# An FFT convolution feeding a mixture of experts: float16 products two token sets earlier, scale loads reordered, second-layer weights split in other groups

## The chip, the core and the metric

The kernel runs on one core of a Trainium2 chip. The metric is the device time of one execution in microseconds; less is better. In the text PE is TensorE's matmul unit and PEld its weight load, DVE is VectorE, ACT is ScalarE, POOL is GpSimd and SP is SyncE, whose queue issues most transfers.

## The reference

A length-2496 real FFT along the sequence is multiplied by a filter and transformed back, for 8 batches of 256 channels. The 19968 rows that come out go through a top-2 mixture of 8 experts.

```python
X = np.fft.rfft(x, axis=1)                                   # x: 8 x 2496 x 256
y = np.fft.irfft(X * (filt_r + 1j * filt_i)[None], n=2496, axis=1)
x = y.reshape(19968, 256)
noisy = x @ w_gate + np.log1p(np.exp(x @ w_noise)) * noise    # 8 experts
top2 = the two largest of noisy; top2_w = softmax over these two
for e in range(8):
    for k in range(2):
        mask = top2[:, k] == e
        h = np.maximum(x[mask] @ w1[e], 0.0)                  # 256 -> 1024
        out[mask] += top2_w[mask, k, None] * (h @ w2[e])      # 1024 -> 256
```

All inputs and the output are float32.

## The kernel before

**Two streams in one program.** `fft_stream` is a generator that emits the FFT, gating and routing of the 8 batches in small steps. `expert` emits the expert products in blocks of 512 gathered rows, and yields 13 times in a block: once after each of the 8 groups `f` of hidden units, once when the next block has been prepared, and once after each of the 4 groups of 128 output rows. `run` puts the two together: after each yield of `expert` it lets `fft_stream` take some steps, by a pace for each set, and it lets the generator `wscales` take some steps too. A scheduler then orders the instructions of each engine by the order of the program and the availability that it computes; engines execute in that order.

**Sets and blocks.** Blocks come in sets; set i may only use the rows of batches 0 to i. `SETS` is 2, 12, 18, 24, 34, 44, 54, 64: set 0 is blocks 0 and 1, set 1 blocks 2 to 11, set 2 blocks 12 to 17, all single blocks with their own expert and weights (n = 1); set 3 is blocks 18 to 23, in pairs that share one expert's weights (n = 2), and so on. Smaller blocks and the prepared weights of the tail follow.

**Splitting a product in three.** Each float32 operand is split into a high and a low part, and `_mm3` (lines 124 to 126) makes three matmuls: high by high, high by low, low by high. A block has 8 groups x 2 halves of the inner dimension x 3 = 48 matmuls of 512 columns in the first layer (into `hps`) and 4 row groups x 8 x 3 = 96 matmuls of 256 columns in the second (into `yps`). Blocks with `ready < HALF` (`ready` is the set's number plus 1) split into parts of the type float32r, the others into scaled float16 parts:

```python
if ent[0][5] >= HALF:
    xT.append(self.pair(h, l, x, self.xs[ent[0][5]][:, 0:1]))   # float16, scaled
else:
    nc.scalar.copy(h, x)                                        # float32r
    nc.vector.tensor_sub(l, x, f32v(h))
```

For w1 the same choice stands in `wsplit` (lines 1316 with 1203 and 1204, or 1322 and 1323), for w2 in lines 1319 and 1320 or 1322 and 1323. With `HALF` at 5, blocks 0 to 23 use float32r and the rest float16.

**The scales** are powers of two. `wscales` finds the weights' scales: 64 loads of 256 KB (`load`, line 598) into two buffers `wp` in turn, each followed two steps later by an ACT instruction that sums squares (`top`, line 603) and, after each fourth, a DVE maximum. Then `powers` turns the sums into scales by a short chain of PE, DVE, PE and DVE (lines 558 to 575, then `wtab`). Then 12 loads of a part of the rows of batches 0 and 1 (`load_y`, line 615) into the same two buffers, with a DVE maximum each (line 620), for the activations' scale. `known` then lets `xscale` run in the FFT stream as soon as a batch is complete; a batch that comes earlier is put on the list `owed`. `run` spreads these 88 steps (`NPREP`) evenly over the first `READY` yields of `expert`, 280 of them, or 21.5 blocks. What is not done by the first float16 block is emitted there: `gather` copies that expert's scales on POOL (line 1149) ahead of the block's row gathers. POOL also scatters the results of the blocks (line 1399).

**w2** arrives in 4 quarters in the staging slots that w1 uses as well; in the first block that uses it each quarter is split on ACT and DVE in the groups f = 1, 3, 5 and 7, behind the group's relu (ACT, line 1371) and low part (DVE, line 1372).

Of the kernel before, what the change touches and what calls it, by code (L numbers as in the profile page):

```python
# [10 lines left out]
F32 = mybir.dt.float32  # L11
# [11 lines left out]
NB, S, D = 8, 2496, 256  # L23
# [110 lines left out]
PACES = 115  # L134
FILL = {0: 0, 1: 14}
RAW = 3
HALF = 5
EVERY = 3
SETS = FIRST + [18 + 2 * n for n in PAIRS[ALONE:]]
READY = 13 * SETS[HALF - 2] - 32  # L140
FIRSTS = 2
NPREP = 8 * E + 2 + 4 + 12 + 2 + 4

# [9 lines left out]
class Moe:  # L153
# [40 lines left out]
    def setup(self):  # L194
        tc, nc, io, cp = self.tc, self.nc, self.io, self.cp
        self.z = cp.tile([128, YW // 2], F32, name="z")
        nc.gpsimd.memset(self.z, 0.0)
        self.ident = cp.tile([128, 128], F32, name="ident")
        make_identity(nc, self.ident)
        self.cV = cp.tile([128, 128], F32, name="cf")  # L200
        hl = cp.tile([128, 732], R32, name="hl")
        self.small = cp.tile([128, 320], F32, name="small")
        self.half = cp.tile([128, 4 * LR + 2 * NG], F16, name="half")
        self.fr = cp.tile([128, 2, 20, 128], F32, name="fr")
        self.fi = cp.tile([128, 2, 20, 128], F32, name="fi")
        self.wg = cp.tile([128, 2, 32], F32, name="wg")
        self.sgn = cp.tile([64, 20], F32, name="sgn")


        self.stage = cp.tile([128, 4096 + 4 * YW], F32, name="stage")  # L210
        self.turns = {}
        self.F = [self.stage[:, 2560 * h:2560 * h + 2560].rearrange("p (k b) -> p k b", k=CB) for h in range(2)]
        cm = self.P.tile([128, 366], F32, name="cm", tag="tl", bufs=3)
        self.cm = cm
        self.rC, self.rM, self.rD = cm[:RP, 0:120], cm[:, 120:248], cm[:120, 248:365]
        self.hl = hl
        nc.vector.memset(self.wg, 0.0)
        self.cC = (hl[:RP, 0:120], hl[:RP, 120:240])
        self.cM = (hl[:, 240:368], hl[:, 368:496])
        self.cD = (hl[:120, 496:613], hl[:120, 614:731])  # L220
        sm = self.small
        self.tri, self.ones, self.key = sm[:, 0:128], sm[:, 128:256], sm[:, 256:264]
        self.lastok, self.iota = sm[:, 264:265], sm[:, 272:272 + SW]
        self.epart, self.ebase, self.eoff = sm[:, 304:305], sm[:, 305:306], sm[:, 306:314]
        self.base = cp.tile([128, E], F32, name="base")
        self.cnt = cp.tile([E, 1], F32, name="cnt")
        self.done = cp.tile([E, 1], F32, name="done")
        self.nblk = cp.tile([E, 1], F32, name="nblk")
        for t in (self.cnt, self.done, self.nblk):
            nc.vector.memset(t, 0.0)  # L230
        self.tab = cp.tile([1, 2, SW], F32, name="tab")
        self.ymax = cp.tile([128, 2 * NB, 6], F32, name="ymax")
        self.xm = cp.tile([128, 1], F32, name="xm")
        self.wmax = cp.tile([128, 2 * E], F32, name="wmax")
        self.wquart = cp.tile([128, 4], F32, name="wquart")
        self.wtab = cp.tile([128, 3, E], F32, name="wtab")
        nc.vector.memset(self.ymax, 0.0)
        self.xs, self.scaled, self.known, self.owed, self.relu = {}, False, False, [], None

        self.rank = [cp.tile([RP, n, E], F32, name=f"rank{n}") for n in (39, 38)]  # L240
        nc.vector.memset(self.rank[0][:, :17], 0.0)
        nc.vector.memset(self.rank[1][:, :16], 0.0)

        self.pre = [cp.tile([128, 4 + E], F32, name=f"pre{i}") for i in range(2)]
        for t in self.pre:
            nc.vector.memset(t[:, :4], 0.0)
# [331 lines left out]
    def xscale(self, bt):  # L578

        nc = self.nc  # L580
        if not self.known:
            self.owed.append(bt)
            return
        nc.vector.tensor_reduce(self.xm, self.ymax[:, :2 * bt + 2], axis=AX.XY, op=ALU.max)
        q = yield from self.powers(self.xm, 1, TX)
        t = self.xs[bt + 1] = self.cp.tile([128, 2], F32, name=f"xs{bt}")
        nc.vector.tensor_copy(t, q[:, :, 0])
        yield

    def wscales(self):  # L590


        nc, io, v = self.nc, self.io, self.nc.vector

        def load(i):
            t = self.P.tile([128, 512], F32, name="wp", bufs=2)
            with self.after(self.spw):
                nc.sync.dma_start(t, io["w1" if i < 4 * E else "w2"][i // 4 % E, i % 4])
            return t

        def top(i, t):
            with self.after(self.relu):
                nc.scalar.activation(t, t, AF.Square, accum_out=self.wquart[:, i % 4:i % 4 + 1])
            if i % 4 == 3:
                v.tensor_reduce(self.wmax[:, i // 4:i // 4 + 1], self.wquart, axis=AX.X, op=ALU.max)

        Y = [(bt, h, g) for bt in range(FIRSTS) for h in range(2) for g in range(0, NG, 8)]

        def load_y(i):
            bt, h, g = Y[i]  # L610
            t = self.P.tile([128, 8, 64], I32, name="wp", bufs=2)
            y = self.y[BLK + bt * ROWS:BLK + (bt + 1) * ROWS].rearrange("(p g) d -> p g d", p=RP)
            k = min(8, NG - g)
            with self.after(self.spw):
                nc.sync.dma_start(t[:RP, :k], y[:, g:g + k, 128 * h + 64:128 * h + 128])
            return t[:RP, :k].rearrange("p g w -> p (g w)").bitcast(BF16)

        def top_y(i, t):
            bt, h, g = Y[i]
            v.tensor_reduce(self.ymax[:RP, 2 * bt + h, g // 8:g // 8 + 1], t, axis=AX.X, op=ALU.max, apply_absolute_value=True)  # L620

        raw, cut = (t.rearrange("p h k d -> p (h k d)")[:, :4096].rearrange("p (s q f) -> p s q f", s=2, q=4) for t in (self.fr, self.fi))

        def load_all(i):
            nc.sync.dma_start(raw[:, i % 2], io["w1" if i < E else "w2"][i % E].rearrange("q p f -> p q f"))

        def split(i, q):
            a, e = i // E, i % E
            o = cut[:, i % 2].rearrange("p q f -> p (q f)").bitcast(F16).rearrange("p (q f) -> p q f", q=4)
            h, l, t = o[:, q, :512], o[:, q, 512:], raw[:, i % 2, q]  # L630
            nc.scalar.activation(h, t, AF.Copy, scale=self.wtab[:, a, e:e + 1])
            v.scalar_tensor_tensor(l, t, self.wtab[:, a, e:e + 1], h, op0=ALU.mult, op1=ALU.subtract)
            if q == 3:
                nc.sync.dma_start(self.wpl[e, a].rearrange("q p f -> p q f"), o)

        def pairs(first, then, n):
            old = []
            for i in range(n + 2):
                if i >= 2:
                    self.pin(then, *old.pop(0), hold=False)  # L640
                if i < n:
                    old.append((i, self.pin(first, i, hold=False)))
                yield

        yield from pairs(load, top, 8 * E)
        for a, t in enumerate((TW1, TW2)):
            q = yield from self.powers(self.wmax[:, a * E:a * E + E], E, t, True)
            v.tensor_copy(self.wtab[:, a], q[:, 0])
            if a == 0:
                v.tensor_copy(self.wtab[:, 2], q[:, 1])  # L650
            else:
                v.tensor_mul(self.wtab[:, 2], self.wtab[:, 2], q[:, 1])
            yield
        yield from pairs(load_y, top_y, len(Y))
        self.known = True
        while self.owed:
            yield from self.xscale(self.owed.pop(0))
        self.scaled = True
        yield
        self.pin(load_all, 0)  # L660
        yield
        for i in range(2 * E):
            if i + 1 < 2 * E:
                self.pin(load_all, i + 1)
            yield
            for q in range(4):
                self.pin(split, i, q)
                if q < 3:
                    yield
# [664 lines left out]
    def expert(self, parts, may, fill=None):  # L1334
# [5 lines left out]
        while self.ahead:  # L1340
# [3 lines left out]
            blk, i = ent[:2]  # L1344
            lt, n, nt, s, tabi, ready = blk
            w = 128 * nt
            w1, xT, w2st, sc = cur
            if i == 0:
                w2, adds = [], []
# [5 lines left out]
            for f in range(8):  # L1355
# [17 lines left out]
                if f == 4:  # L1373
                    self.early_l = v
                hh.append((h, l))
                if f % 2 and i == 0:
                    w2.append(self.wsplit(w2st[f // 2], "w2", sc))
                yield
            late = not self.ahead
            if late:  # L1380
# [146 lines left out]
```

## Time and profile before

| | |
|---|---|
| time, median of 3 runs | 2170.51 us (2169.66 to 2174.63) |
| the profiled execution's own time | 2164.38 us |
| its span, first to last instruction | 2162.5 us |
| mean granted TensorE clock | 0.991 of full speed |
| PE busy | 2095.9 us, 97% |
| PEld busy | 1595.5 us, 74% |
| DVE busy | 1466.3 us, 68% |
| ACT busy | 1286.1 us, 59% |
| POOL busy | 1029.2 us, 48% |

The profile is of one execution. A matmul's recorded duration overlaps the next one's, so PE at 97% says that matmuls follow each other almost without a break; how fast they follow is read from the distance of their starts. "Idle before" an instruction is idle time of its engine, with what ended it. Times of rows below count from the span's start.

### The profile page before, as it was taken

The page shows a single profiled execution, that of the slowest core. Times are in us where ns is not written, and L with a number is a line of the kernel's source. Part 1 is how long each engine was busy: PE and PEld are TensorE (multiplying, and loading weights), DVE is VectorE, ACT ScalarE, POOL GpSimd, SP SyncE. Part 2 cuts the span into 40 slices and gives each one's busy share as a digit, 9 for nine tenths or more (in the row PEclk, how much of TensorE's full clock was granted, in tenths as well). Part 3 has the DMA queues.
Part 4 walks back from the last instruction along what each step waited for, and adds up shares of the span by engine and source line. Part 5 has one row for each costly group of instructions (what it writes and reads, how often), then busy time and mean ns, then how long its engine had stood idle before and what let it go on. Part 6 is the DMA issues. An engine that isn't in the chain of part 4 may idle for free. (4 is left out here: it accounts for less than half of the span.)

```text
span 2162.5 us, 42794 instructions
## 1 busy us (share of the span) xinstructions
PE 2095.9 (97%) x14517; PEld 1595.5 (74%) x14517; DVE 1466.3 (68%) x3221; ACT 1286.1 (59%) x2505; POOL 1029.2 (48%) x946
## 2 busy tenths in 40 slices
PE   8779999999999999999999999999999999999997
PEld 6447988888888888766766676666666666667886
DVE  5866779877978886678665986589666664333443
ACT  6666866786577446656664565555566564333443
POOL 4233334434544344445444453555655665654563
PEclk9989999999999999999999999999999999999999
DMA  9588989999999775767766687666889999869997
GB/s 255 165 259 223 222 223 215 252 228 228 223 214 233 161 156 137 178 150 183 155 156 131 152 182 165 146 121 132 233 210 240 240 249 234 170 142 229 276 280 175
DMA packets 511673, 428.48 MB, mean 198 GB/s; under 512 B 215679, under 2 KB 397015, under 8 KB 511447
## 3 DMA queue, kind: packets, MB, share of 16 engines
q1 hardware_dynamic: 450135, 341.27, 60.2%
q0 software_dynamic: 61312, 84.40, 23.1%
q8 instruction: 116, 1.90, 0.4%
q14 instruction: 110, 0.90, 0.1%
HBM read 263.92 MB, written 122.03 MB: 178 GB/s over the span
## 5 line engine op out<-in xcount | busy, mean ns | idle before, releaser
L1372 DVE SCALAR_TENSOR_TENSOR hl<-hps,hh 128x512 f16<-128x512 f32 (+3 forms) x712 | 432.4, 623 | 356.6 <-ACT hh L1371 354.7
L1399 POOL DMA_INDIRECT out<-stage,ids x316 | 532.9, 1686 | 270.4 <-ACT stage L1398 167.0
L1158 POOL DMA_INDIRECT stage<-y,ids x316 | 347.9, 1101 | 535.7 <-DMA xt<-stage 433.9
L124 PE MATMUL yps<-w,hh 128*128 128x256 f16 (+1 forms) x2048 | 556.5, 278 | 5.2 <-ACT stage L1398 3.4
L125 PE MATMUL yps<-w,hh 128*128 128x256 f16 (+1 forms) x2048 | 551.2, 277 | 0.0
L126 PE MATMUL yps<-w,hl 128*128 128x256 f16 (+1 forms) x2048 | 541.9, 277 | 1.8 <-DVE hl L1372 1.5
L1371 ACT ACTIVATE hh<-hps 128x512 f16<-128x512 f32 (+3 forms) x712 | 376.7, 550 | 198.9 <-PE hps L126 183.8
L125 PE MATMUL hps<-mxl,w1h 128*128 128x512 f16 (+1 forms) x1024 | 394.4, 386 | 2.2 <-DVE mxl L1246 1.3
L126 PE MATMUL hps<-mxh,w1l 128*128 128x512 f16 (+1 forms) x1024 | 394.0, 386 | 0.0
L124 PE MATMUL hps<-mxh,w1h 128*128 128x512 f16 (+1 forms) x1024 | 385.6, 388 | 5.1 <-DVE hl L1372 5.1
L1398 ACT ACTIVATE stage<-yps,gt 128x256 f32<-128x256 f32 x316 | 143.1, 475 | 329.0 <-PE yps L126 202.0
L124 PEld LDWEIGHTS <-hh 128*128 128x128 f16 x1760 | 172.2, 98 | 52.4 <-issue 6.2
L126 PEld LDWEIGHTS <-hl 128*128 128x128 f16 x1760 | 171.5, 98 | 47.9 <-DVE hl L1372 1.9
L125 PEld LDWEIGHTS <-hh 128*128 128x128 f16 x1760 | 172.2, 98 | 34.2 <-issue 2.6
L124 PEld LDWEIGHTS yps<-w,hh 128*128 128x128 f32 x768 | 145.8, 190 | 12.5 <-ACT stage L1398 2.2
L126 PEld LDWEIGHTS yps<-w,hl 128*128 128x128 f32 x768 | 145.0, 190 | 10.3 <-issue 1.7
L125 PEld LDWEIGHTS yps<-w,hh 128*128 128x128 f32 x768 | 145.4, 191 | 4.6
L126 PEld LDWEIGHTS <-w1l 128*128 128x128 f16 x640 | 62.6, 98 | 71.8 <-issue 1.5
L541 ACT COPY yt<-q 117x1024 uint16<-117x1024 uint16 x96 | 90.9, 947 | 40.7 <-PE q L535 32.1
L1228 DVE COPY stage<-xt 128x1024 uint16<-128x1024 uint16 (+2 forms) x174 | 109.0, 679 | 1.4 <-DMA xt<-stage 1.4
L124 PEld LDWEIGHTS <-w1h 128*128 128x128 f16 x640 | 62.4, 98 | 51.5 <-issue 5.5
L125 PEld LDWEIGHTS <-w1h 128*128 128x128 f16 x640 | 62.6, 98 | 51.1 <-issue 3.0
(286 smaller groups left out, 4024.4 us busy)
## 6 DMA issues: line engine op xcount, KB each, us to landing
stage<-w SPq DMA_DIRECT2D x328, 256.0 KB
x<-x SPq DMA_DIRECT2D x88, 256.0 KB
fd<-c SPq DMA_DIRECT2D x77, 240.0 KB
fi<-wpl SPq DMA_DIRECT2D x18, 1024.0 KB
fx<-fd SPq DMA_DIRECT2D x140, 128.0 KB
out<-z SPq DMA_DIRECT2D x24, 702.0 KB
wp<-w SPq DMA_DIRECT2D x64, 256.0 KB
fr<-w SPq DMA_DIRECT2D x16, 1024.0 KB
```

Source lines behind the costliest of these rows:

```text
L124: nc.tensor.matmul(o, lh, rh, start=start, stop=False)
L125: nc.tensor.matmul(o, lh, rl, start=False, stop=False)
L126: nc.tensor.matmul(o, ll, rh, start=False, stop=stop)
L541: e = nc.scalar.copy(yt.bitcast(U16)[:, :k, :256].rearrange("p g (two d) -> p g two d", two=2), p.bitcast(U16)[:RP, :2 * m].rearrange("p ( ...
L1158: self.pin(lambda: nc.gpsimd.indirect_dma_start(out=x.bitcast(I32), out_offset=None, in_=self.y[:BLK + ready * ROWS], in_offset=bass.Indir ...
L1228: nc.vector.tensor_copy(xu.rearrange("p (t two) -> p two t", two=2), ent[3][0][:, 2 * kc:2 * kc + 2, :w])
L1371: self.relu = hold(lambda: nc.scalar.activation(h, p, AF.Relu))
L1372: v = hold(lambda: nc.vector.scalar_tensor_tensor(l, p, 0.0, hf[0], op0=ALU.max, op1=ALU.subtract))
L1398: nc.scalar.activation(o, p, AF.Copy, scale=gate[:, t])
L1399: a = nc.gpsimd.indirect_dma_start(out=self.io["out"][:BLK + ready * ROWS], out_offset=bass.IndirectOffsetOnAxis(ap=ids[:, t:t + 1], axis= ...
```

## The change

- `HALF` goes from 5 to 3: blocks 12 to 23 (sets 2 and 3) are multiplied in float16 parts too.
- `READY` goes from 280 to 78: the 88 steps of `wscales` are spread over the first 78 yields, 6 blocks.
- In `wscales` the 12 loads for the activations' scale, `known` and the batches owed come ahead of the 64 loads of the weights' sums.
- The activations' scales stand in one tile `xst` in place of a tile each.
- In single blocks of four row groups the quarters of w2 are split in the groups f = 0, 1, 2 and 3; in pairs as before.

```diff
-HALF = 5
+HALF = 3
 EVERY = 3
 SETS = FIRST + [18 + 2 * n for n in PAIRS[ALONE:]]
-READY = 13 * SETS[HALF - 2] - 32
+READY = 13 * SETS[HALF - 2] - 78
...
+        self.xst = cp.tile([128, NB, 2], F32, name="xst")
...
-        t = self.xs[bt + 1] = self.cp.tile([128, 2], F32, name=f"xs{bt}")
+        t = self.xs[bt + 1] = self.xst[:, bt]
...
+        yield from pairs(load_y, top_y, len(Y))
+        self.known = True
+        while self.owed:
+            yield from self.xscale(self.owed.pop(0))
         yield from pairs(load, top, 8 * E)
         for a, t in enumerate((TW1, TW2)):
             q = yield from self.powers(self.wmax[:, a * E:a * E + E], E, t, True)
...
-        yield from pairs(load_y, top_y, len(Y))
-        self.known = True
-        while self.owed:
-            yield from self.xscale(self.owed.pop(0))
         self.scaled = True
...
-                if f % 2 and i == 0:
-                    w2.append(self.wsplit(w2st[f // 2], "w2", sc))
+                q = (f if f < 4 else None) if n == 1 and nt == 4 else f // 2 if f % 2 else None
+                if q is not None and i == 0:
+                    w2.append(self.wsplit(w2st[q], "w2", sc))
```

## Rows read from the trace of the kernel before

**Rows 1.** Windows by stage: length, busy us (instructions) of PE, PEld, DVE, ACT, POOL; PEclk, DMA share, GB/s

```profile
163.00:202.00 39.00, 36.90 (x236) 31.30 (x236) 26.04 (x58) 23.98 (x49) 13.94 (x12) 1.00 0.81 210
202.00:351.00 149.00, 147.16 (x941) 129.49 (x939) 114.43 (x244) 109.38 (x229) 59.97 (x54) 0.99 0.94 225
351.00:533.00 182.00, 179.95 (x1176) 158.21 (x1176) 142.38 (x286) 135.75 (x283) 73.54 (x62) 1.00 0.98 232
533.00:890.00 357.00, 346.18 (x2262) 303.16 (x2261) 283.03 (x636) 221.83 (x435) 153.21 (x123) 1.00 0.82 190
890.00:1158.00 268.00, 265.29 (x1851) 183.19 (x1852) 196.27 (x406) 170.43 (x310) 124.64 (x111) 1.00 0.70 158
```

**Rows 2.** PE timeline, four unbroken runs, first and last row: start, duration

```profile
698.17 0.40 PE L125 MATMUL hps<-mxl,w1h 128*128 128x512 f32 x1
...
701.66 0.39 PE L126 MATMUL hps<-mxh,w1l 128*128 128x512 f32 x1
...
735.24 0.28 PE L124 MATMUL yps<-w,hh 128*128 128x256 f32 x1
...
741.11 0.28 PE L125 MATMUL yps<-w,hh 128*128 128x256 f32 x1
...
1382.33 0.38 PE L125 MATMUL hps<-mxl,w1h 128*128 128x512 f16 x1
...
1385.78 0.38 PE L126 MATMUL hps<-mxh,w1l 128*128 128x512 f16 x1
...
1976.25 0.27 PE L124 MATMUL yps<-fi,hh 128*128 128x256 f16 x1
...
1981.38 0.27 PE L126 MATMUL yps<-fi,hl 128*128 128x256 f16 x1
```

**Rows 3.** Groups by line and form: count | busy us, mean ns | idle before, releasers

```profile
L1204 DVE SCALAR_TENSOR_TENSOR w1l<-stage,sc,w1h 128x512 f16<-128x512 f32 x80 | 59.6, 744 | 52.9 <-ACT w1h L1203 52.4 <-issue 0.4
L1323 DVE TENSOR_TENSOR w1l<-stage,w1h 128x512 fp32r<-128x512 f32 x84 | 57.9, 693 | 15.2 <-ACT w1h L1322 15.1
L1203 ACT ACTIVATE w1h<-stage,sc 128x512 f16<-128x512 f32 x80 | 57.5, 718 | 40.3 <-PE hps L125 38.9 <-DMA fr<-w 0.8 <-DMA y<-yt 0.5
L1322 ACT CAST w1h<-stage 128x512 fp32r<-128x512 f32 x84 | 52.2, 626 | 35.6 <-DMA stage<-w 27.2 <-PE hps L125 8.0
```

**Rows 4.** Wait for the y loads (us, times, longest); window of nine of these loads

```profile
DVE ymax L620 <- DMA wp<-y: 16.5, 8, 4.5
...
695.00:728.00 33.00, 30.38 (x210) 25.30 (x209) 22.24 (x34) 15.15 (x33) 9.28 (x8) 1.00 0.85 195
```

**Rows 5.** Window of line 603 alone: length, ACT busy us (two instructions a load)

```profile
202.00:351.00 149.00, 14.87 (x42) 0.99 0.94 225
```

**Rows 6.** Groups by line, ACT, 202 to 351 us: four of these to a block

```profile
L1398 ACT ACTIVATE stage<-yps,gt 128x256 f32<-128x256 f32 x20 | 9.1, 480 | 15.1 <-PE yps L126 11.1 <-issue 3.9
```

**Rows 7.** SP and ACT timelines: two weight loads issued, and the sums that they release

```profile
176.41 0.34 SPq L598 DMA_DIRECT2D wp<-w  x1
...
179.10 0.63 ACT L603 ACTIVATE wp<-wp 128x512 f32<-128x512 f32 x1
...
515.51 0.52 SPq L598 DMA_DIRECT2D wp<-w  x1
...
519.91 0.63 ACT L603 ACTIVATE wp<-wp 128x512 f32<-128x512 f32 x1 [1.46 <-DMA wp<-w]
```

**Rows 8.** Waits of SP's queue: us, times, longest

```profile
SPq L598 <- ACT wp L603: 43.8, 21, 5.7
```

**Rows 9.** Timelines: batch 2's last maximum, block 12's first gather, scale chain's start, its POOL reader

```profile
421.17 0.41 DVE L546 TENSOR_REDUCE ymax<-yt 117x1 f32<-117x256 bf16 x1
...
468.03 1.44 POOL L1158 DMA_INDIRECT stage<-y,ids  x1 [0.58 <-POOL ids L1108]
...
804.75 0.27 PE L558 MATMUL xm<-ident,wmax 128*8 128x128 f32 x1
...
837.79 0.44 POOL L1149 COPY sc<-wtab 128x3 f32 x3 [8.22 <-DVE wtab L652]
```

## The prediction, as put on record

> **What bounds the kernel now.** I read the windows by stage first: one row for a stretch of the block sequence, with PE's busy time beside its length. From 202 to 1158 us PE is busy in all but 1 to 3% of each stretch, DVE in 73 to 79% and ACT in 62 to 75%; the granted clock is 0.99 to 1.00, the upper of its two levels [rows 1]. So PE sets the pace, and an edit pays where it makes PE's instructions fewer or closer together. A recorded matmul lasts longer than its share of PE, so the second view is PE's timeline: in an unbroken run the distance of the starts is the cost. The reader is to divide first-to-last by the number of steps. The third question is where the change puts new work beside PE: in the early blocks, where ACT already has 109.4 of 149 us and the transfer engines are in use for 0.94 of the time [rows 1].
>
> **The float16 products.** In float32r, 15 steps of 512 columns take 701.66 - 698.17 = 3.49 us, 233 ns each, and 49 steps of 256 columns 5.87 us, 120 ns each. In float16, 16 steps of 512 take 3.45 us, 216 ns, and 47 steps of 256 take 5.13 us, 109 ns [rows 2]. The difference is 17 ns and 10.7 ns. Twelve blocks, 12 to 23, change over; each has 48 matmuls of the first kind and 96 of the second. 576 x 17.1 = 9.8 us and 1152 x 10.7 = 12.3 us, together 22.1 us less. These matmuls stand on PE in a stretch of 357 us in which it is idle for 10.8 [rows 1], so the saving is on the path as long as the other engines follow. The lower end is nothing, if another engine takes over at once; the upper end adds the idle time that the float16 stretch behind doesn't have (2.7 us in 268, so 3.4 in 335 in place of 10.8): 7.4 more, 29.5 in all.
>
> The Trainium skill (page "TensorE: Matmul & The Clock Gate", section "Wait — 56ns, not 53.3ns?") gives the start-to-start distance of warm matmuls as columns over 2.4 GHz plus about 2.5 ns, without a word on the operands' type. The float16 rows, 216 and 109 ns, agree with it; the float32r rows, 233 and 120 ns, do not. By that rule the whole 22.1 us would be nothing; I go by the rows.
>
> **What float16 splitting costs elsewhere.** A float16 high part takes ACT 718 ns against 626, a low part DVE 744 against 693 [rows 3]. Blocks 12 to 23 have 9 weight loads (6 single, 3 pairs) of 8 quarters, and 24 halves of the rows: 96 splits, 96 x 92 = 8.8 us of ACT and 96 x 51 = 4.9 us of DVE. Cover: ACT is idle 135 us and DVE 74 us of those 357 [rows 1]. Shortened by 22 us, the stretch would still have DVE at 288 of 335, 86%. Counted as nothing; if that cover were gone, up to 4.9 us. The two more runs of `xscale` (some ten tiny DVE instructions each; even at 0.74 us each 15 us) and the gate and scale copies on POOL (busy 153 of 357 [rows 1]) sit in the same cover.
>
> **The loads for the activations' scale, moved early.** Before, DVE waited 16.5 us for 8 of these 12 loads: the maximum stood in DVE's order before its data was there. The stretch with nine of them has PE idle for 2.6 of 33 us [rows 4]. That goes, and comes back in blocks 0 and 1, where DVE has 26.0 of 39 us and PE idles 2.1 already [rows 1]. I count the two against each other: nothing, between -2.6 and, if PE pays for all of the wait, 13.9.
>
> **The weights' sums, moved close together.** Each load's two ACT instructions take 14.87 / 21 = 0.71 us [rows 5]. Steps 15 to 80 of the 88 now fall on yields 13 to 71, so 64 loads in 58 yields, 4.4 blocks. Five blocks take the 149 us from 202 to 351 (20 evictions, four to a block [rows 6]), so one load comes every 2.05 us. ACT's demand there becomes 109.4 - 14.9 + 64 x 0.71 = 140 of 149 us: it fits, barely. The second limit is the pair of buffers. A load may be issued when the sum two before it is done, so in two intervals, 4.1 us, an issue (0.5), a landing and a sum (0.7) must fit: 2.9 us for the landing. The rows show 516.03 to 519.91, 3.9 us, with ACT waiting for it, and 176.75 to 179.10, at most 2.4 [rows 7]. Halfway, 3.15, is 0.25 too long, 32 pairs times: 8 us in which ACT stands still, with no slack left, so I put them on PE. From both sides: nothing, if the sums slide into later blocks (they aren't needed before block 12), and 32 us at 3.9. Each load's issue also waits in SP's queue for that sum, 43.8 us in 21 waits before [rows 8]; behind it stand the weights' and x loads and the row transposes, and a late transpose delays the next gathers on POOL. I keep that inside the 32.
>
> In return blocks 6 to 15 lose 43 sums and 11 MB of loads. PE idles 2.1 us from 351 to 533 [rows 1]; I count 2 us back, between 0 and 4.
>
> **w2 in groups 0 to 3.** The same ACT and DVE instructions, four groups earlier, in 18 single blocks. The staging slots come free sooner; ACT waited 27.2 us for staged weights before w1's high part [rows 3], but PE did not. Against it, groups 0 to 3 carry a split and a relu each: one DVE instruction in PE's way a block would be 18 x 0.69 = 12 us. I take nothing; -2 to 12.
>
> **The sum.** -22.1 + 8 - 2 = -16.1 us. From the profiled execution's own 2164.4 us that is 2148.3. The median of the runs shown lies 6.1 us above that execution, so 2154.4: I say 2154.
>
> **The rivals.** About 0.2% (4 us) is what a measurement of this kernel can tell from no change.
>
> *More comes free* (chance 0.15). The float16 blocks run as smoothly as those from 890 us on and the sums find room: -29.5 - 2 = -31.5, 2139. For it: PE idle time of 1% there. Against it: DVE's share rises to 86%.
>
> *ACT runs full early* (0.10, slower). Landings as long as the longer one in rows 7, because more bytes come in the same time: -22.1 + 32 - 2 + 13.9 with the early y loads would be +22, 2192; without the latter 2178. It decides from a landing of some 3.7 us on, where 32 x 0.8 passes the gain. For it: transfers at 0.94 already. Against it: nothing needs the sums before block 12's gather at 468 [rows 9], over 100 us behind.
>
> *The weights' scales come late* (0.09, slower). Before, the chain of `powers`, emitted at yields 210 to 223 (about 645 us by its block), began at 804.75 and ended 33 us later, and POOL stood still 8.2 us for it [rows 9]: 160 us of lag, I take it behind the FFT steps that were emitted before it and whose PSUM banks it shares. Now it is emitted at yield 73, about 337 us. With the same lag it ends at 530, but block 12's first gather stood at 468.03 [rows 9], with the copy of the scales ahead of it on POOL; behind that copy stand the scatters of blocks 10 and 11, whose eviction slots are four. A 62 us hold less the 25 us that one block's slack covers is 37: +21, 2191. It decides from a hold of about 45 us on. Against it: batch 2, whose steps it is emitted among, was through at 421 [rows 9], so a chain behind it should be done by 455.
>
> *The FFT sets the end of set 3* (0.07, no change). Block 24 waits for batch 4. If the FFT's own engines, not PE, time it, the 22 us are waited away: 2164.4 + 6 + 6.1 = 2176 with the sums' cost, 2168 without, of which I take the latter. DVE at 79% speaks against.
>
> *The type makes no difference to PE* (0.01). If 233 and 120 ns came from the surroundings and not from the type, the sum is +6: 2176. In rows 2 both kinds run unbroken. The rule of the Trainium skill's page "TensorE: Matmul & The Clock Gate", weighed above, would give this.
>
> **The numbers.** The forecast as it stands, 2144 to 2164, has 0.58. Range: from 2136, below the case in which more comes free, to 2182; left out are the two slower cases at their worst and a still larger gain, together 2 in 10. Faster: 0.58 + 0.15, less 0.01 at the edge, 0.72; the same 0.08; slower 0.20.
>
> **What would show it.** The matmuls of blocks 12 to 23 with f16 in their forms, 216 and 109 ns apart; the stretch from block 12 to block 24 at some 335 in place of 357 us. ACT at over 0.9 from 202 to 351 us, waits of line 603 for `wp`, and blocks 1 to 5 some 8 us longer. DVE waits of line 620 below 205 us. POOL's first copy of the scales without a long wait. The prediction is wrong if blocks 0 to 11 grow by over 20 us, if POOL waits over 45 us for `wtab`, or if the stretch of blocks 12 to 23 keeps its length although its matmuls are closer.

## The result and the profile after

The change made the kernel slower: 2198.7 us (median of 4 runs, 2193.8 to 2200.3) against 2172.6 for the kernel before on the same chip, a ratio of 1.0114 (95% interval 1.0094 to 1.0133), some 25 us by the ratio. The forecast was 2154 with a range of 2136 to 2182. The profiled executions differ by more, 2197.1 and 2162.5 us of span, since that of before lies some 8 us under its median and that of after at its own.

Windows by stage of the kernel after, to be read against [rows 1]; columns as there. The cuts are those of the blocks: 163 to 195 us holds block 0, 195 to 370 us blocks 1 to 5, then come 6 to 11, 12 to 17, 18 to 23 and 24 to 33.

```profile
163.00:195.00 32.00, 30.39 (x197) 25.93 (x197) 29.78 (x59) 17.29 (x34) 6.29 (x3) 1.00 0.88 212
195.00:370.00 175.00, 154.56 (x932) 129.80 (x931) 113.56 (x215) 128.24 (x284) 63.02 (x60) 0.99 0.96 247
370.00:552.00 182.00, 176.45 (x1125) 154.07 (x1125) 139.32 (x321) 120.69 (x242) 83.63 (x69) 0.98 0.90 203
552.00:727.00 175.00, 165.19 (x1134) 111.68 (x1133) 143.62 (x321) 114.86 (x213) 77.71 (x72) 0.97 0.80 184
727.00:917.00 190.00, 176.61 (x1203) 121.33 (x1202) 142.97 (x319) 116.48 (x213) 74.83 (x67) 0.96 0.69 161
917.00:1179.00 262.00, 261.31 (x1809) 179.67 (x1808) 195.11 (x403) 167.01 (x305) 128.29 (x112) 1.00 0.74 164
```

PE now idles 20.4 us in blocks 1 to 5, 9.8 us in blocks 12 to 17 and 13.4 us in blocks 18 to 23, and the granted clock falls to 0.97 and 0.96 in these last two. In blocks 1 to 5 ACT is busy for 0.73 of the time, the DMA share is 0.96 and the rate 247 GB/s (0.94 and 225 in [rows 1]). The matmuls themselves did what was forecast. PE's timeline of the kernel after, two unbroken runs in block 13, first and last row of each:

```profile
598.90 0.38 PE L124 MATMUL hps<-mxh,w1h 128*128 128x512 f16 x1
...
600.85 0.38 PE L126 MATMUL hps<-mxh,w1l 128*128 128x512 f16 x1
601.06 0.27 PE L124 MATMUL yps<-w,hh 128*128 128x256 f16 x1
...
605.43 0.27 PE L125 MATMUL yps<-w,hh 128*128 128x256 f16 x1
```

Nine steps in 1.95 us are 217 ns each, 40 steps in 4.37 us are 109 ns, as in the float16 rows of [rows 2]. What went wrong stands in the waits of the kernel after (us, times, longest); line 604 is the sum that was 603 before, 599 its load, 621 the maximum over the y loads, 588 the copy of an activations' scale.

```profile
ACT wp L604 <- DMA wp<-w: 37.0, 29, 4.1
...
PE q L510 <- DVE xst L588: 8.0, 1, 8.0
...
DVE ymax L621 <- DMA wp<-y: 4.6, 4, 1.8
...
SPq L599 <- ACT wp L604: 27.4, 25, 4.0
```

ACT stands still 37.0 us for weight loads. DVE waits 4.6 us for the y loads instead of the 16.5 of [rows 4]. SP waits for the sums less than in [rows 8] (43.8). ACT's window of line 604 alone (length, ACT busy us and instructions):

```profile
195.00:370.00 175.00, 35.78 (x99) 0.99 0.96 247
```

That is 0.72 us a load, near the 0.71 of [rows 5]. The pair of buffers is seen in the SP and ACT timelines of one of the two, four sums and the three loads between them (rows of other instructions and of the other buffer are left out), against [rows 7]:

```profile
313.72 0.63 ACT L604 ACTIVATE wp<-wp 128x512 f32<-128x512 f32 x1 [0.26 <-DMA wp<-w]
314.47 0.33 SPq L599 DMA_DIRECT2D wp<-w  x1
318.89 0.63 ACT L604 ACTIVATE wp<-wp 128x512 f32<-128x512 f32 x1 [0.39 <-DMA wp<-w]
319.64 0.34 SPq L599 DMA_DIRECT2D wp<-w  x1
323.51 0.63 ACT L604 ACTIVATE wp<-wp 128x512 f32<-128x512 f32 x1
324.61 0.52 SPq L599 DMA_DIRECT2D wp<-w  x1
329.14 0.63 ACT L604 ACTIVATE wp<-wp 128x512 f32<-128x512 f32 x1 [0.92 <-DMA wp<-w]
```

The load is issued when the sum has freed the buffer, and the next sum runs 4.1 and 4.0 us after the issue's end in the two cases where ACT waited for it (314.80 to 318.89, 325.13 to 329.14). Three turns take 15.42 us, 5.14 each for two loads, where the prediction's rate allowed 4.1. The stretch is one of the quicker ones. ACT's timeline has the first and the last of the 64 sums here:

```profile
220.35 0.63 ACT L604 ACTIVATE wp<-wp 128x512 f32<-128x512 f32 x1 [4.11 <-DMA wp<-w]
...
407.08 0.65 ACT L604 ACTIVATE wp<-wp 128x512 f32<-128x512 f32 x1
```

So the 64 sums take 186.7 us, one in 2.96, and a turn is 5.9 us in the mean. Over the 29 sums for which ACT waited, the time from the end of a load's issue to its sum is 4.0 us in the mean, between 2.3 and 5.2.

The scales of the weights were in time. Timelines of the kernel after: batch 2's last maximum, block 12's first gather, the start of the chain that makes the weights' scales, POOL's copy of them, against [rows 9]:

```profile
472.37 0.41 DVE L547 TENSOR_REDUCE ymax<-yt 117x1 f32<-117x256 bf16 x1
...
486.62 1.03 POOL L1159 DMA_INDIRECT stage<-y,ids  x1 [0.16 <-POOL ids L1109]
...
499.80 0.28 PE L559 MATMUL xm<-ident,wmax 128*8 128x128 f32 x1
...
521.72 0.44 POOL L1150 COPY sc<-wtab 128x3 f32 x3 [0.50 <-DVE wtab L657]
```

POOL waited 0.5 us for them. But batch 2 is complete 51 us later than before, and all later batches are late as well. The following table gives, from the timelines, the first relu of blocks 6, 12 and 24, the last maximum over batches 2 and 4, and the end, all counted from the first relu of block 0. It has those experiments too that are read against each other; the first column of numbers is the ratio to the kernel before on the same chip.

| kernel | ratio | block 6 | batch 2 | block 12 | batch 4 | block 24 | end |
|---|---|---|---|---|---|---|---|
| before | 1 | 183.2 | 257.9 | 364.2 | 679.5 | 721.1 | 1998.8 |
| after | 1.0114 | 207.9 | 310.0 | 388.8 | 724.9 | 754.2 | 2034.3 |
| e1, order alone | 1.0151 | 205.8 | 309.0 | 390.2 | 726.2 | 755.0 | 2044.0 |
| e2, after, no sums | 0.9943 | 187.6 | 264.1 | 372.1 | 673.6 | 705.6 | 1993.2 |
| e3, before, no sums | 0.9994 | 183.7 | 256.7 | 365.1 | 683.9 | 724.9 | 2007.3 |
| e5, sums, no loads | 0.9999 | 195.2 | 295.3 | 370.3 | 708.2 | 737.6 | 2022.1 |
| e6, loads, no sums | 1.0052 | 213.9 | 289.3 | 398.0 | 705.0 | 736.6 | 2028.8 |
| e7, e2 and no y loads | 0.9909 | 184.0 | 257.0 | 367.3 | 666.5 | 697.7 | 1990.1 |
| e15, 32 of 64 loads | 0.9972 | 195.5 | 269.7 | 377.2 | 681.4 | 714.3 | 2006.3 |
| e16, 16 of 64 loads | 0.9914 | 190.3 | 263.6 | 373.7 | 674.3 | 703.5 | 1985.7 |

Two distances in the table show where the loss is carried on. Batch 4 is complete 409 to 417 us after batch 2 in all rows but those of before and e3 (422 and 427), and block 24 starts 29 to 33 us after batch 4 in all but these two (41.6 and 41.0). So in these rows block 24 comes when the FFT lets it, and it is about as late as batch 2. The first distance is not a fixed time of the FFT, though: it is 401 us in e17, 407 in e11, 368 in e8 and 381 to 396 in e13 and e14, which are not in the table. The end of set 2 looks alike: block 18 starts 31 us after batch 3 (82 before). What the 29 us hold, and how the loss looks at the hand-over, DVE's timeline of the kernel after shows:

```profile
887.25 0.41 DVE L547 TENSOR_REDUCE ymax<-yt 117x1 f32<-117x256 bf16 x1
...
896.07 1.58 DVE L1321 SCALAR_TENSOR_TENSOR w<-stage,sc,w 128x512 f16<-128x512 f32 x2
905.68 1.35 DVE L1229 COPY stage<-xt 128x1024 uint16<-128x1024 uint16 x2 [8.03 <-DMA xt<-stage]
906.93 0.74 DVE L1321 SCALAR_TENSOR_TENSOR w<-stage,sc,w 128x512 f16<-128x512 f32 x1
907.58 0.16 DVE L588 COPY xst<-xm 128x2 f32<-128x2 f32 x1
```

Batch 4's last maximum ends at 887.66; then block 24's rows are gathered and transposed. DVE's order has the copy of these rows (line 1229) ahead of the copy of the scale (line 588), so DVE waits 8.03 us for the transpose, and the FFT's next transposes (line 510), which need the PSUM bank of the scale's chain, wait behind it. PE's timeline and windows at that place (window columns as above):

```profile
899.38 0.40 PE L348 MATMUL q<-xl,hl 117*120 117x512 f32 x1
907.79 1.11 PE L510 MATMUL q<-ident,G 128*120 128x128 f32 x4 [8.02 <-DVE xst L588]
...
909.55 0.63 PE L534 MATMUL q<-th,hl 120*117 120x512 f32 x1
...
910.83 0.63 PE L348 MATMUL q<-xl,hl 117*120 117x512 f32 x1
```

```profile
890.00:900.00 10.00, 9.55 (x78) 8.02 (x75) 5.95 (x9) 7.41 (x14) 5.61 (x6) 1.00 0.42 96
900.00:910.00 10.00, 2.21 (x8) 1.87 (x9) 4.32 (x8) 3.23 (x7) 8.20 (x8) 0.63 0.95 219
910.00:917.00 7.00, 7.00 (x29) 3.56 (x27) 3.35 (x6) 2.47 (x5) 3.67 (x6) 0.79 0.93 205
```

PE idles 8.02 us. The granted clock is 1.00 ahead of it, 0.63 in the window that holds it and 0.79 in the busy 7 us behind: after the idle time PE works at its lower level, 1.2 GHz, for a while (three steps of 512 columns in 1.28 us, 427 ns each). At that place PE pays for the wait twice. Over the whole execution the granted clock is 0.984 (0.991 before); what that costs in all is not worked out here.

### The profile page after: what moved, and what is told of

Read it like the earlier page. It is cut to its first block, busy times and chain, and to the rows that moved or that the text cites. A ratio compares the mean times of both kernels' runs of the same rounds, so it can differ in the third digit from the quotient of the medians.

```text
span 2197.1 us, 42902 instructions
## 1 busy us (share of the span) xinstructions
PE 2096.9 (95%) x14527; PEld 1519.7 (69%) x14527; DVE 1472.8 (67%) x3241; ACT 1296.3 (59%) x2505; POOL 1026.7 (47%) x967
## 4 chain that ended last, share of the span: by engine, by line
PE 78%; DMA 7%; ACT 6%; DVE 4%; issue 4%; SPq 1%; POOL 0%; POOLq 0%; ACTq 0%; DVEq 0%
PE hps L124 11%; PE hps L125 11%; PE hps L126 11%; PE yps L126 11%; PE yps L124 11%; PE yps L125 11%; DMA wp<-w 3%; PE q L449 2%; PE q L510 1%; PE u L462 1%; ACT wp L604 1%; DMA stage<-w 1%; PE q L338 1%; DVE hl L1373 1%; ACT yt L542 1%
## 5 line engine op out<-in xcount | busy, mean ns | idle before, releaser
L124 PEld LDWEIGHTS <-hh 128*128 128x128 f16 x2144 | 210.1, 98 | 64.6 <-issue 7.5
L126 PEld LDWEIGHTS <-hl 128*128 128x128 f16 x2144 | 209.3, 98 | 61.4 <-issue 4.9
L125 PEld LDWEIGHTS <-hh 128*128 128x128 f16 x2144 | 210.3, 98 | 43.0 <-issue 4.4
L126 PEld LDWEIGHTS <-w1l 128*128 128x128 f16 x832 | 81.7, 98 | 95.7 <-issue 4.0
L125 PEld LDWEIGHTS <-w1h 128*128 128x128 f16 x832 | 81.7, 98 | 73.6 <-issue 10.4
L124 PEld LDWEIGHTS <-w1h 128*128 128x128 f16 x832 | 81.5, 98 | 71.8 <-issue 10.2
L1205 DVE SCALAR_TENSOR_TENSOR w1l<-stage,sc,w1h 128x512 f16<-128x512 f32 x116 | 86.2, 746 | 65.7 <-ACT w1h L1204 48.6
L1204 ACT ACTIVATE mxh<-stage,xst 128x512 f16<-128x512 f32 (+2 forms) x154 | 101.6, 661 | 29.8 <-PE hps L126 16.0
L1204 ACT ACTIVATE w1h<-stage,sc 128x512 f16<-128x512 f32 x116 | 83.0, 719 | 61.3 <-PE hps L125 35.3
L1205 DVE SCALAR_TENSOR_TENSOR mxl<-stage,xst,mxh 128x512 f16<-128x512 f32 (+2 forms) x154 | 103.9, 676 | 15.8 <-ACT mxh L1204 13.4
```

What stands on the lines that cost most here:

```text
L124: nc.tensor.matmul(o, lh, rh, start=start, stop=False)
L125: nc.tensor.matmul(o, lh, rl, start=False, stop=False)
L126: nc.tensor.matmul(o, ll, rh, start=False, stop=stop)
L1204: self.nc.scalar.activation(h, x, AF.Copy, scale=s)
L1205: self.nc.vector.scalar_tensor_tensor(l, x, s, h, op0=ALU.mult, op1=ALU.subtract)
```

## Experiments

The theory at first: the early sums make ACT wait for their loads, because two buffers give a load too little time; the waits lengthen the early blocks and push the FFT back. The rivals: the sums' ACT time alone does it, whatever the loads; the y loads or the groups of w2 do it; or float16 has no saving to give.

The edits are given against the kernel after unless another is named.

**Order alone, and the groups of w2.** e1 has the new order and place of the loads and nothing else; e4 is the kernel before with the last hunk of the change alone, the groups of w2; e12 is after with before's groups.

```diff
-HALF = 3          # e1, with READY at 78 as after
+HALF = 5
-                q = (f if f < 4 else None) if n == 1 and nt == 4 else f // 2 if f % 2 else None   # e1, e12
+                q = f // 2 if f % 2 else None
```

> The kernel before with the loads' new order and the 88 steps spread over 78 yields, but float16 only from set 4 on and w2 split in its old groups. Squeeze theory (64 sums in 58 yields fill ACT and outrun the two buffers): blocks 0 to 11 grow by 20 to 28 us, ACT waits for wp 30 to 40 us, the whole kernel takes 2190 to 2200. Hand-over theory (the float16 blocks outrun the FFT, which then sets the ends of sets 2 and 3): blocks 0 to 11 may grow, but without float16 blocks most of the loss is regained later, 2170 to 2182.

Measured: 1.0151 (1.0092 to 1.021). So the new order and place of the loads cost all of it, with float32r in blocks 12 to 23; float16 took almost nothing off the start of block 24 (755.0 and 754.2 in the table).

> The kernel before with nothing but the new groups for w2. Both theories: within 4 us of before. A third theory, that the splits in groups 0 to 3 hold up the relus of the single blocks: 5 to 12 us more, in blocks 0 to 17.

Measured: 0.9999 (0.9975 to 1.0023).

> The changed kernel with w2 split in its old groups. If the new groups cost nothing under a full ACT either: 2194 to 2204, like the changed kernel. If four splits in the first groups are what delays the relus there: 2175 to 2190.

Measured: 1.0136 (1.0105 to 1.0168), as after within the intervals. The groups of w2 cost or give nothing that these runs can tell, some 5 us.

**No sums.** e2 takes the 64 loads and sums out of the kernel after, e3 out of the kernel before; the weights' scales then come from a constant. e7 also leaves the y loads out of e2, so that batches 0 and 1 don't count in the activations' scales.

```diff
+        nc.vector.memset(self.wmax, 0.25)
-        yield from pairs(load, top, 8 * E)
+        for _ in range(8 * E + 2):
+            yield
```

> The changed kernel without the 64 weight loads and their sums of squares (the weights' scale comes from a constant instead, so that part of the computation is left out). Squeeze theory: blocks 0 to 11 are back at the length of before (block 12 near 525 us), and the float16 gain shows: 2140 to 2152. Hand-over theory: blocks 18 and 24 still wait for the rows of batches 3 and 4, which leaves 2160 to 2172.

Measured: 0.9943 (0.9918 to 0.9968). The sums cost the kernel after 1.0114 - 0.9943, some 37 us; by the two intervals that is known to some 7 us.

> The kernel before without the 64 weight loads and their sums (constant scale, that part left out): the base line for the run above. Both theories: the sums were spread so thin that they cost little, 2160 to 2170.

Measured: 0.9994 (0.9968 to 1.0019): the same 64 sums, spread over 21 blocks, cost the kernel before nothing that shows. So without sums on either side the rest of the change is worth 0.9994 - 0.9943, some 11 us (each ratio is known to some 5 us).

> The changed kernel without the 64 loads and sums and without the 12 loads of rows for the activations' scale (batches 0 and 1 don't count for it; constant weights' scale). If these 12 loads in blocks 0 and 1 cost what the blocks 0 to 11 of the run without sums had over those of before without sums (7 us): 2150 to 2154, and no DVE wait on line 621's maximum. If that was something else: 2156 to 2162.

Measured: 0.9909 (0.9885 to 0.9933). The y loads cost 4.8 us in blocks 0 to 11 by the profiles (372.1 and 367.3); the intervals of the totals overlap.

**Which half of the sums.** e5 keeps the sums and leaves out the loads (it sums fixed tiles); e6 keeps the loads and has ACT copy one column of each in place of the sum (constant scales again, and no maxima of the sums).

```diff
-        yield from pairs(load, top, 8 * E)                                      # e5
+        fixed = [self.P.tile([128, 512], F32, name="wp", bufs=2) for _ in range(2)]
...
+        yield from pairs(lambda i: fixed[i % 2], top, 8 * E)
-                nc.scalar.activation(t, t, AF.Square, accum_out=...)            # e6
+                nc.scalar.copy(self.wquart[:, i % 4:i % 4 + 1], t[:, :1])
```

> The changed kernel with the 64 sums kept on ACT, but on two tiles that are filled once with ones in place of the 64 loads (the weights' scale then comes from these ones). Capacity theory (ACT's 45 us of sums in blocks 1 to 6 are too much): most of the 40 us between the changed kernel and the one without sums stays, 2180 to 2195, block 12 near 545 us. Landing theory (ACT stands in order behind sums whose loads haven't landed): 2155 to 2168, block 12 near 537.

> The changed kernel with the 64 loads kept, but each sum of 512 squares replaced by an ACT copy of one column, which waits for the same landing (constant weights' scale, sums left out). Landing theory: ACT still waits some 35 us for wp, 2185 to 2200. Capacity theory: ACT has 30 us less to do, 2160 to 2170.

Measured: e5 0.9999 (0.9986 to 1.0012), e6 1.0052 (1.0033 to 1.0071). Over e2 that is 12 and 24 us, together 36 of the 37: the two halves add up as far as the intervals, some 6 us on each difference, can tell. They act at different places. Windows of e5 over most of its blocks 0 to 5, then of e6, and e6's wait:

```profile
161.00:350.00 189.00, 175.94 (x1088) 151.85 (x1088) 136.60 (x248) 149.16 (x341) 68.42 (x60) 0.98 0.82 190
```

```profile
163.00:370.00 207.00, 182.89 (x1106) 156.65 (x1105) 142.66 (x266) 121.98 (x274) 66.11 (x59) 0.96 0.96 245
```

```profile
ACT wquart L605 <- DMA wp<-w: 62.9, 39, 7.7
```

In e6 ACT is busy for 122 of 207 us and waits 62.9 us: blocks 0 to 5 take 26.3 us longer than in e2 (213.9 and 187.6). In e5 ACT is busy for 149 of 189 us and there is no load to wait for: blocks 0 to 5 take 7.6 us longer, but batch 2 falls behind them, 100.1 us after block 6 where e2 and e6 have 76.5 and 75.4. In the kernel after both come together: 20.3 us and 25.6 us (102.1 against 76.5) make batch 2's 45.9 over e2, and block 24 is 48.6 later.

**More distance for all 64 loads.** A load every 0.9 yields in the kernel after (78 over 88) becomes one every 0.95 to 2.3. e8, e9, e10 and e11 have the old order (weights' sums first), e13 and e14 the new one; e11, e13 and e14 have float16 from block 18 on. In e8 every chain of `powers` and in e13 that of the weights has the expert's bank `xps` instead of a shared one.

```diff
-READY = 13 * SETS[HALF - 2] - 78
+READY = 84        # e10; 100 in e9, 124 in e8, 150 in e11, 165 in e14, 205 in e13
-HALF = 3
+HALF = 4          # e11, e13, e14
```

> The changed kernel with the loads in the order of before and spread over 124 yields, as the offset of before would have it, and the PSUM tile of the scale chain taken from the bank of the third expert product instead of the FFT's three. If the dense loads are the whole loss and the chain's lag came from waiting behind the FFT's tiles: 2146 to 2160, the weights' table done within 40 us of its last sum. If the chain lags for another reason, POOL waits for the table at block 12: 2175 to 2200.

> The changed kernel with the loads in the order of before (sums, table, then the 12 loads of rows) over 100 yields: 64 loads in 73 yields instead of 58, beginning with block 0. A pair of loads then has some 5.2 us, which leaves 4.0 for a landing. Landing theory: the waits for wp fall from 37 to under 15 us and blocks 0 to 11 regain 10 to 20 us; the sums' ACT time still delays the FFT, so blocks 18 and 24 still wait: 2165 to 2180. If it is the number of sums alone and not their spacing: 2190 to 2200.

> The same order over 84 yields: 64 loads in 61 yields, nearly the spacing of the changed kernel, but begun in block 0 and with the 12 loads of rows behind them. Landing theory: waits for wp of 25 to 40 us, 2180 to 2195. If the order (rows first) was what hurt: 2160 to 2175.

> Float16 from set 3 on only (blocks 18 to 23 change over), loads in the order of before over 150 yields, one weight load in 1.7 yields. Half the matmul saving, 11 us, with hardly a wait for wp (under 10 us): 2158 to 2168 if the FFT keeps up; if block 24 still waits for batch 4, the saving goes there: 2168 to 2175.

> Only set 3 (blocks 18 to 23) goes over to float16, the 88 steps are spread over 205 yields in place of 78 (2.3 yields to a load; 1.3 in the kernel after, in the new order, the sums' end some 10 blocks in), and the two chains that turn sums into scales have a PSUM bank of their own; w2 and the order of the loads as in the kernel after. If the loss comes from the short distance between a load and its sum: ACT's waits for wp fall below 15 us (37.0 in the kernel after), the FFT keeps its lead at blocks 12 to 24, and what stays is half of the float16 saving, 11 us, less the 5 us of the early y loads: 2155 to 2166, faster than before. If the early position of the sums as such pushes the FFT back, whatever the spacing: waits of 30 us and more and 2170 to 2190.

> As the run before it in the list, with the 88 steps over 165 yields (1.9 to a load) and the chains in the shared banks. If distance decides: ACT's waits for wp between 10 and 25 us, 2160 to 2172. If not: 2175 to 2190 and waits of over 30 us.

Measured:

| | yields to a load | ACT's waits for `wp`, us (times) | ratio, interval |
|---|---|---|---|
| after | 0.9 | 37.0 (29) | 1.0114 (1.0094 to 1.0133) |
| e10 | 0.95 | 35.0 (25) | 1.0096 (1.0059 to 1.0133) |
| e9 | 1.1 | 39.1 (29) | 1.0132 (1.0106 to 1.0158) |
| e8 | 1.4 | 55.0 (22) | 1.0352 (1.0319 to 1.0386) |
| e11 | 1.7 | 46.6 (20) | 1.0022 (1.0005 to 1.0039) |
| e14 | 1.9 | 30.3 (11) | 0.9997 (0.9977 to 1.0016) |
| e13 | 2.3 | 41.1 (12) | 1.0068 (1.0041 to 1.0095) |

(The expectation of e13 gives 1.3 yields for the kernel after; it is 0.9.) My theory that the distance of load and sum decides fell: the waits become fewer and longer, and their sum follows no order. (These runs differ from each other in order, banks and float16 blocks too.) Where one of e13's two longest comes from is seen in its SP and ACT timelines:

```profile
580.18 0.34 SPq L604 DMA_DIRECT2D wp<-w  x1
...
586.15 3.87 SPq L1203 DMA_TRANSPOSE xt<-stage  x1
...
594.59 1.19 SPq L1203 DMA_TRANSPOSE xt<-stage  x1
...
596.51 1.08 SPq L604 DMA_DIRECT2D wp<-w  x2
```

```profile
590.25 0.83 ACT L1405 ACTIVATE stage<-yps,gt 128x256 f32<-128x256 f32 x2
602.27 0.63 ACT L609 ACTIVATE wp<-wp 128x512 f32<-128x512 f32 x1 [11.19 <-DMA wp<-w]
```

The load stands in SP's queue behind four row transposes and is issued at 596.51; ACT has come to its sum at 591 and does nothing for 11.19 us. More distance in the program doesn't help where the queue of the loads is held up and the engine that sums goes in order. What then follows in e13 (its blocks 12 to 17 take 210.0 us) I have not taken apart. e8 says little: block 12 began only at 651.5 us. I put that down to the chain of the activations' scales, which is emitted in the FFT stream and now used the expert's bank; no run shows it. In e9 block 12 waited for an activations' scale that was ready at 568.5; e10 is no better. That the kernel before, with 3.2 yields to a load, waits only 5.9 us in 3 cases is thus not explained by distance alone; this stays open.

**Fewer loads.** e15 keeps every second load and sum, e16 every fourth, over the same yields; an expert's scale then comes from two or from one of its matrix's four quarters. e17 is e16 with the weights' loads first, one in two steps, and the y loads behind them.

```diff
-        yield from pairs(load, top, 8 * E)
+        old = []                                   # e16
+        for i in range(3, 8 * E + 8, 4):
+            if i >= 11:
+                self.pin(top, *old.pop(0), hold=False)
+            if i < 8 * E:
+                old.append((i, self.pin(load, i, hold=False)))
+            for _ in range(4 if i < 8 * E else 1):
+                yield
```

> The kernel after with every second of the 64 weight loads and sums left out (the weights' scales then come from half of the quarters); the 58 yields stay, so each load has twice the distance to its sum, and the bytes and ACT's time for sums halve. If the waits come from the distance of load and sum: ACT's waits for wp fall from 37.0 us to under 8, blocks 0 to 11 take under 375 us (388.8 after, 372.1 without any sums), and the total is 2160 to 2178. If each load brings its wait whatever the distance: waits of 15 to 20 us, half of the loss, 2177 to 2183.

> The kernel after with 16 of the 64 weight loads and sums (one quarter of each expert's matrix, from which its scale is then taken), still over the same yields. Halving the loads took the total from some 40 us above the kernel without sums to some 13 above it. If what is left follows the waits: ACT waits for wp at most 3 times, blocks 0 to 11 in 368 to 374 us, the total 0.993 to 0.997 of the kernel before, faster. If something else of the change costs the rest (the early y loads, the scales' chains): no better than the run with half the loads, 0.997.

> As the run before it in the list, with the order of the kernel before: the 16 weight loads first, one in two steps, and the 12 loads of y behind them, some two blocks later than in the kernel after. If the y loads cost some 5 us because they fall into the few blocks in which the FFT and the expert's first blocks need DVE: 3 to 6 us less than its neighbour, 0.990 to 0.995. If their place does not matter: the same as its neighbour within 3 us.

Measured: e15 0.9972 (0.9953 to 0.9992), e16 0.9914 (0.9899 to 0.9929), e17 0.994 (0.9926 to 0.9955). e15's ACT still waits 26.1 us in 9 cases, more than either theory said, but batch 2 is only 5.6 us later than in e2, and the loss falls from 37 to some 6 us: where ACT has half of the sums to do, most of its waits cost little. e16 is faster than both kernels: 2147.0 us against 2166.0 on its chip. Its waits and its windows, blocks 1 to 5, 12 to 17 and 18 to 23:

```profile
ACT wp L605 <- DMA wp<-w: 7.3, 1, 7.3
```

```profile
195.00:352.00 157.00, 148.41 (x932) 129.59 (x931) 117.60 (x255) 105.86 (x216) 71.39 (x60) 0.98 0.91 219
...
536.00:696.00 160.00, 152.86 (x1067) 104.63 (x1067) 138.71 (x308) 107.69 (x199) 80.17 (x71) 1.00 0.89 198
696.00:866.00 170.00, 168.91 (x1190) 116.26 (x1188) 137.29 (x313) 110.69 (x206) 73.34 (x66) 1.00 0.71 161
```

ACT has 105.9 of 157 us in place of 128.2 of 175, and PE idles 1.1 us in blocks 18 to 23 in place of 13.4. e17 is no faster than e16: the profiled spans are 2148.0 and 2147.9, the medians 2151.5 and 2147.0. A gain of 3 us from the later y loads does not show, but e17's weight loads also stand twice as close, so it does not price the y loads alone.

## Why the prediction was wrong

**The float16 products: right.** The distances are 217 and 109 ns. The rule of the Trainium skill (page "TensorE: Matmul & The Clock Gate", section "Wait — 56ns, not 53.3ns?") fits these rows; that the type makes no difference, which it would have given, is refuted by them. With few sums the saving is there: from block 12 to block 24 e16 takes 329.8 us and before 356.9, 27 us less, of which 6 go back by block 34 (605.8 and 626.8 from block 12 to 34, 21.0 less); the term was 22.1, its upper end 29.5. In the kernel after itself the saving did not arrive.

**The weights' sums: the step that failed, +8 where the chip paid some 37.** The landing was taken halfway between the two rows, 3.15 us. It was 4.0 in the mean over the 29 for which ACT waited: about the longer of the two rows, which the rival "ACT runs full early" took. The turn of a buffer was 5.1 to 5.9 us in place of 4.1, and ACT stood still for 37.0 us: the upper bound of 32, not 8, was near the value. ACT did not run full as that rival and the first sign had it: it was busy for 0.73 of blocks 1 to 5, not over 0.9, and stood still in between. And a wait is not its own price: e15's 26.1 us of waits went with a loss of some 6 us, e6's 62.9 with 24. The Trainium skill (page "DMA: Bandwidth & Descriptors", section "Anatomy of one DMA — SWDGE (gpsimd) path") fits a DMA with some 2.0 us plus its bytes over 436 GB/s. As an estimate by this page 256 KB would take 2.6 us and fit the turn; these loads go by SP, in traffic of 247 GB/s in all, and the rows decide.

**What was not priced.** I put ACT's lost time on PE, as if the two streams stopped together. The FFT stopped longer than the blocks, since ACT's time for the sums ("it fits, barely") displaced its instructions: e5, without any wait for a load, has batch 2 late by 31 us. In no run does block 24 begin earlier than some 28 us after batch 4, and before had 41.6: of the 22 us only some 13 could be taken unless batch 4 comes earlier too. In e16 both are seen: block 24 comes 17.6 us earlier than before, 5.2 of them by an earlier batch 4. The rival "the FFT sets the end of set 3" saw this and got 0.07; it and "ACT runs full early" (0.10) were counted as exclusive, but they came together: the hand-over is as short without the loss (32 us in e2, 29 in e16), and the sums push batch 4 itself back. Two of the three signs that I had set for a wrong prediction appeared: blocks 0 to 11 grew by 24.6 us, and blocks 12 to 23 took 365.4 us in place of 356.9 although their matmuls are closer.

**The y loads: 0 was a little low**, some 5 us by e2 and e7, within the bound of 13.9. DVE's wait fell from 16.5 to 4.6 us, but the price is paid in blocks 0 and 1, as feared. Their windows in before, after, e2 and e7 (columns as above):

```profile
163.70:230.30 66.60, 62.95 (x389) 54.40 (x388) 42.91 (x86) 41.48 (x85) 25.96 (x24) 0.97 0.88 219
162.80:237.20 74.40, 65.05 (x405) 54.95 (x403) 55.10 (x98) 41.20 (x83) 26.20 (x23) 1.00 0.90 222
164.50:235.50 71.00, 62.70 (x381) 53.33 (x379) 54.81 (x97) 36.95 (x70) 25.00 (x23) 0.98 0.89 208
163.40:229.80 66.40, 61.88 (x388) 54.61 (x386) 42.70 (x85) 37.50 (x71) 26.86 (x25) 0.97 0.79 188
```

They take 74.4 us in place of 66.6, and PE idles 9.4 in place of 3.7; with the y loads alone (e2) 71.0, without them (e7) 66.4. DVE has 12 us more to do there. (The row from 163 to 202 us that the prediction reads as blocks 0 and 1 is block 0 alone: block 1 begins at 202.1.) **w2: right**, nothing that shows in e4 and e12. **The scales in time: right**, POOL waits 0.5 us. Their chain starts at 499.80, long behind its place in the program, as the rival had it (with before's lag, 337 + 160, it would start near 497); but POOL's order has the copy behind block 12's first gathers, at 521.7 in a block that starts at 551.6, and not ahead of them, so it holds nothing. **Given back, 2 us:** not seen; blocks 6 to 11 take 180.9 us and took 181.0.

The sum as it came, from block to block in the profiles: +24.6 for blocks 0 to 11, +8.5 for 12 to 23, +2.4 behind, +35.5. The totals of several runs say 25, since the profiled execution of before is one of its fastest.

## What to carry to other kernels

When two streams share engines and one hands work to the other, price a stall twice: in the stream where it stands, and in how late the other stream then hands over; the slack at each hand-over (here some 13 us) is the most that a faster consumer can take while the producer comes no earlier. A ring of two buffers has a turn of issue, landing and use; size it by the longest landing in the trace, not by the middle, when the edit adds traffic. Look also at how much time the waiting engine has left, since a wait costs little where it has slack (e15). If a statistic only has to choose a power of two, ask how much of the data it needs before asking where to hide the loads: a quarter of them was worth more here (e16, 0.9914) than any spacing that was tried (at best 0.9997).

## What the runs showed of the hardware

A 256 KB load took 4.0 us in the mean (29 loads, 2.3 to 5.2) from the end of its issue to the instruction that waited for it while 247 GB/s moved; [rows 7] had 3.9 and at most 2.4. An idle time of PE of 8.0 us left a granted clock of 0.63 in the window that holds it and 0.79 in the next 7 us, after 1.00 ahead of it; no term of the prediction had that. Spreading the same 64 loads over 0.9 to 2.3 yields each made ACT's waits fewer (from 29 to 11 or 12) and the longest of them longer (4.1 us, and 5.5 to 11.5 from 1.4 yields on); their sum stayed between 30 and 55 us.
